# First rows' norm on ScalarE, postponed weight stores, output weights loaded in rows, separate PSUM kinds, and a planner that knows a shared port and longer DMA times

## The chip, the cores and the metric

The kernel runs on one core of a Trainium2 chip. Five engines work side by side, each on its own queue in program order: TensorE (PE; its weight loads are listed as PEld), VectorE (DVE), ScalarE (ACT), GpSimd (POOL) and SyncE (SP), which issues all DMAs here. Data lies in SBUF (128 partitions) and TensorE writes to PSUM, which has eight banks of 128 x 512 float32. The metric is the device time of one execution in microseconds; the time before is the median of three runs.

## What is computed

Two layers, each an attention block with a compressive memory and a Fourier mixing block, on x of 2048 rows by 512, in float32:

```python
for layer in range(2):
    x = x + A(layernorm(x))     # 32 heads of 16, four segments of 512 rows
    x = x + B(layernorm(x))

# A, per segment s, with q, k, v from wq, wk, wv and phi(t) = t + 1 if t > 0 else exp(t)
p = softmax(q_s @ k_s.T / 4 + causal mask)
a_mem = (phi(q_s) @ M) / (phi(q_s) @ z + 1e-6)
o_s = g * a_mem + (1 - g) * (p @ v_s)
M, z = M + phi(k_s).T @ v_s, z + sum(phi(k_s))
# then all o_s @ wo

# B
y = dft_seq_re @ (x @ dft_hid_re.T) - dft_seq_im @ (x @ dft_hid_im.T)
```

## The kernel before

**Numbers.** Products are made in float16 with each operand split into a high and a low half: three matmuls (high x high, high x low, low x high) stand for one. Every weight is scaled by a power of two from its absolute maximum first (`scales`, `split`, `split2`): maximum by VectorE, a transpose and a small matmul with ones on TensorE, a few operations on bits on VectorE; then ScalarE makes the high half, and VectorE or GpSimd the low half by a subtraction.

**Units of work.** Heads go in four groups of eight (`NG`), so a layer has 4 segments x 4 groups and the kernel 32 group units (`NGRP`). For a unit i:

- `s_p` projects queries and keys, `s_v` values; results go to a PSUM bank of kind `pj`, and `t_split` brings them to SBUF (ScalarE the high half, VectorE the low half), from where DMAs through DRAM (`d`) reorder them into `qst` and `kst` (three of each, `NR`).
- `s_x` makes all scores once to take each row's maximum (`t_max` on VectorE). They come in ten steps of 512 columns; the two halves of a step run side by side in two PSUM banks.
- `s_st` makes the transposed scores in ten more steps; `t_sel` takes the exponential (ScalarE) and masks (GpSimd).
- `s_av` multiplies with the values in two banks of kind `av`; `t_merge` transposes, divides by the denominators and is also used for the memory part (`s_mem`).
- `s_m` joins both parts into `ot`; after the four groups of a segment `s_o` multiplies with `wo`.

The mixing block takes over row by row: `s_ab` multiplies with the hidden matrices `wd`, `s_r` and `s_c` load and scale the sequence matrices, and `s_f` accumulates into `y`, one bank of kind `dft` at a time. The last quarter of the second layer uses sums of matrix blocks (`t_sums`, with the helper `ttw`) to save products (`t_win`).

**Order.** Nothing in the source says in which order these run. Each stage is a generator that yields what it needs next (`need`: engines, tiles read, PSUM or SBUF kinds to allocate). A planner (`class Plan`) estimates for every engine when it is free and for every tile when it is written and read, from costs per operation (`op`); the main loop always advances the generator that can go first. The instruction queues of the chip are written in that order once, before the run; on the chip each engine follows its queue and waits on semaphores. So a changed cost in `op` removes or adds no instruction and can still reorder all of them. `gate` holds a generator until named stages are planned; `tt` chooses between VectorE and GpSimd by the planned times.

**Slots.** PSUM's eight banks and 52 SBUF slots are lent by kind. `dict(pj=(1, 4), ...)` gives each kind a lowest number that others have to leave it and a highest number. `slots_free` says when a kind can have a bank. Before, maxima, scores and the small transposes of `scales` all use kind `ss`, (2, 6), and past four held `ss` banks two more must stay free.

**The first rows and weights.** Four tiles of x are loaded, then the query and key weights of groups 0 and 1 (into rows of `y`, used as a stage). `t_ln` normalises a row tile: statistics on VectorE, a power -0.5 on GpSimd (`rs`), the normalisation by a VectorE `tensor_scalar`, the high half on ScalarE, the low half on GpSimd or VectorE, and a transposing DMA into `xt`. `s_w` scales the weights: maxima of four pieces, `scales(0, 4)`, four parts, each followed by a store of the split weight to DRAM (`wqkv`, read again for later segments); when the first four row tiles are done it loads the value weights and the rest and goes on with `scales(4, 9)`. The first value projection needs that.

**The output weights.** `s_wo` loads `wo` (1 MB) with one DMA and `wd` (2 MB) with another once their stage rows are free, takes twelve maxima on VectorE, makes two scales one after the other, and splits 4 + 8 pieces.

Of the kernel before, what the change touches and what calls it, by code (L numbers as in the profile page):

```python
# [17 lines left out]
L = S // NSEG  # L18
# [22 lines left out]
AGAIN, LEAN = 0.0, 8.0  # L41
# [5 lines left out]
class Plan:  # L47
# [4 lines left out]
    def __init__(self):  # L52
# [6 lines left out]
        self.fresh = set()  # L59
        self.fine = {}  # L60
# [30 lines left out]
    def slots_free(self, kinds):  # L91
        extra, taken, r = {}, {}, 0.0
        for k in kinds:
# [14 lines left out]
            if k == "ss" and n >= 4:  # L108
                keep += 2
# [37 lines left out]
    def op(self, eng, name, args, kw):  # L147
# [61 lines left out]
        self.free[eng] = e  # L209
        if eng == "T":  # L210
# [47 lines left out]
def body(ctx: ExitStack, tc: tile.TileContext, x, wq, wk, wv, wo, beta, wd, cs, out):  # L258
# [141 lines left out]

    def s_w():
        def part(n, g, how):
# [123 lines left out]
    def t_ln(src, xi, dst, key, row=None):  # L526
# [4 lines left out]
        V.tensor_scalar(mv[:, 2:3], mv[:, 1:2], 1e-5, 2.0 ** -20, op0=OP.add, op1=OP.mult)  # L531
        yield need("G", mv)
        rs = rg("rs", 6, F32, (128, 1))
# [47 lines left out]
    def t_merge(e, o, gi, g, n, key):  # L581
# [843 lines left out]
```

## Time and profile before

| | |
|---|---|
| median of three runs | 1702.74 us (1701.61 to 1703.35) |
| the profiled execution | 1701.07 us |
| its span, first to last instruction | 1699.4 us |
| instructions | 32946 |
| mean granted TensorE clock | 0.986 |
| DMA traffic | 228.16 MB, 134 GB/s |

Times in views of the trace count from the span's start. All instructions but a few carry line 251, that of the helper that records them, so groups are told apart by the names of their tiles: `w` stands for any SBUF slot, `b` for a PSUM bank, `g` for `xt`, `amax` and `scl` for maxima and scales. A row of the order of time gives its start, how long it lasts, engine, line, operation, what it writes and reads, its form, how many are merged in it, and in brackets how long the engine was idle before and what ended that.

### The profile page before, as it was taken

The page shows a single profiled execution, that of the slowest core. Times are in us where ns is not written, and L with a number is a line of the kernel's source. Part 1 is how long each engine was busy: PE and PEld are TensorE (multiplying, and loading weights), DVE is VectorE, ACT ScalarE, POOL GpSimd, SP SyncE. Part 2 cuts the span into 40 slices and gives each one's busy share as a digit, 9 for nine tenths or more (in the row PEclk, how much of TensorE's full clock was granted, in tenths as well). Part 3 has the DMA queues.
Part 4 walks back from the last instruction along what each step waited for, and adds up shares of the span by engine and source line. Part 5 has one row for each costly group of instructions (what it writes and reads, how often), then busy time and mean ns, then how long its engine had stood idle before and what let it go on. Part 6 is the DMA issues. An engine that isn't in the chain of part 4 may idle for free.

```text
span 1699.4 us, 32946 instructions
## 1 busy us (share of the span) xinstructions
PE 1634.7 (96%) x11324; PEld 765.8 (45%) x11324; DVE 1176.6 (69%) x3630; ACT 865.5 (51%) x1433; POOL 839.2 (49%) x1287
## 2 busy tenths in 40 slices
PE   4988899999999999999899999999999999999999
PEld 2443343444445343444444444344444443444488
DVE  6887777778777877456488876857686765552266
ACT  3657656756654556544365664455445444430341
POOL 6547545555554554444345554334643533472672
PEclk9999899999999999999999999999999999999999
DMA  8673546535356433345856664334345331335263
GB/s 206 174 183 91 154 108 157 153 109 163 106 131 183 141 119 100 113 118 170 241 153 182 187 178 116 86 101 130 86 112 145 91 73 63 100 87 169 90 184 118
DMA packets 221272, 228.16 MB, mean 134 GB/s; under 512 B 113072, under 2 KB 139696, under 8 KB 221104
## 3 DMA queue, kind: packets, MB, share of 16 engines
q1 hardware_dynamic: 221104, 226.06, 47.7%
q8 instruction: 89, 1.46, 0.4%
q14 instruction: 79, 0.65, 0.1%
HBM read 140.51 MB, written 61.87 MB: 119 GB/s over the span
## 4 chain that ended last, share of the span: by engine, by line
PE 79%; DVE 7%; DMA 4%; ACT 4%; issue 3%; POOL 2%; SPq 1%; POOLq 0%; ACTq 0%; DVEq 0%
PE b L251 79%; ACT w L251 4%; DMA w<-w 2%; DVE w L251 2%; DVE junk L251 2%; POOL w L251 1%; DMA w<-in_cs_dram 1%; SPq L251 1%; DVE y L251 1%; DVE cam L251 1%; DVE bst L251 0%; DVE mx L251 0%; DMA y<-in_wv_dram 0%; DVE amax L251 0%; DMA kst<-d 0%
## 5 line engine op out<-in xcount | busy, mean ns | idle before, releaser
L251 PEld LDWEIGHTS <-w 128*128 128x128 f16 x5280 | 491.1, 98 | 570.8 <-issue 100.0
L251 PE MATMUL b<-w,w 128*128 128x512 f16 (+1 forms) x3360 | 698.5, 359 | 2.6 <-POOL w L251 1.0
L251 POOL TENSOR_TENSOR w<-w,w 128x512 f16<-128x512 f32 (+3 forms) x356 | 397.0, 1125 | 285.7 <-ACT w L251 246.0
L251 ACT ACTIVATE w<-b,fac 128x512 f32<-128x512 f32 x664 | 408.8, 695 | 174.3 <-PE b L251 173.6
L251 DVE CUSTOM_DVE_ANT_0 junk<-b,cmask 128x256 bf16<-128x256 f32 (+3 forms) x1024 | 437.1, 483 | 56.5 <-PE b L251 55.9
L251 POOL TENSOR_SCALAR_AFFINE_SELECT w<-w 128x256 f32<-128x256 f32 (+1 forms) x640 | 230.0, 368 | 284.8 <-ACT w L251 270.4
L251 DVE SCALAR_TENSOR_TENSOR y<-b,fyu,y 128x512 f32<-128x512 f32 (+1 forms) x296 | 202.1, 688 | 194.5 <-PE b L251 193.9
L251 ACT ACTIVATE w<-w,csu 128x512 f16<-128x512 f32 x320 | 225.5, 720 | 99.0 <-DVE csu L251 48.6
L251 ACT ACTIVATE w<-w 128x512 f16<-128x512 f32 (+2 forms) x160 | 99.5, 626 | 226.4 <-DVE w L251 179.0
L251 PE MATMUL b<-g,w 128*128 128x512 f16 x768 | 186.8, 386 | 3.3 <-DMA g<-w 2.6
L251 PE MATMUL b<-wd,w 128*128 128x512 f16 x768 | 181.5, 382 | 0.7 <-DMA w<-w 0.7
L251 PE MATMUL b<-w,vt 128*32 128x512 f32 (+3 forms) x2048 | 167.7, 450 | 0.2
L251 ACT ACTIVATE w<-b 128x512 f16<-128x512 f32 (+1 forms) x128 | 76.4, 598 | 151.3 <-PE b L251 143.7
L251 DVE SCALAR_TENSOR_TENSOR w<-b,w 128x512 f16<-128x512 f32 x120 | 82.1, 685 | 81.4 <-ACT w L251 81.3
L251 PE MATMUL b<-kst,qst 62*128 62x256 f16 (+3 forms) x1024 | 113.8, 302 | 11.6 <-ACT w L251 4.0
L251 POOL TENSOR_TENSOR w<-w,dn 128x256 f32<-128x256 f32 x109 | 66.3, 628 | 105.8 <-DVE dn L251 84.7
L251 PE MATMUL b<-qst,kst 64*128 64x512 f16 (+3 forms) x1024 | 113.5, 304 | 4.5 <-DVE mx L251 2.0
L251 PE MATMUL b<-w,g 128*128 128x128 f16 x1536 | 97.4, 222 | 5.7 <-DMA w<-w 2.2
L251 PEld LDWEIGHTS b<-w,vt 128*32 128x32 f32 x2048 | 59.9, 111 | 87.2 <-issue 59.0
L251 PEld LDWEIGHTS <-g 128*128 128x128 f16 x1536 | 90.7, 99 | 17.6 <-issue 11.8
L251 DVE STREAM_TRANSPOSE w<-b 128x512 f32<-128x512 f32 x112 | 74.2, 695 | 20.4 <-PE b L251 20.2
L251 PE MATMUL b<-wo,w 128*128 128x512 f16 x384 | 85.5, 379 | 0.0
(101 smaller groups left out, 1000.8 us busy)
## 6 DMA issues: line engine op xcount, KB each, us to landing
w<-in_cs_dram SPq DMA_DIRECT2D x160, 256.0 KB, 3.4
cc<-w SPq DMA_DIRECT2D x128, 256.0 KB, 2.7
w<-cc SPq DMA_DIRECT2D x112, 256.0 KB, 3.3
w<-w SPq DMA_DIRECT2D x96, 256.0 KB, 3.2
d<-w SPq DMA_DIRECT2D x128, 128.0 KB, 2.5
w<-in_x_dram SPq DMA_DIRECT2D x32, 256.0 KB, 3.7
qst<-d SPq DMA_DIRECT2D x64, 128.0 KB, 2.7
kst<-d SPq DMA_DIRECT2D x64, 128.0 KB, 2.9
```

The source lines that it names most:

```text
L251: r = f(*args, **kw)
```

## The change

1. **First rows.** For the four tiles of the first segment of the first layer, the normalisation goes to ScalarE, as an Identity activation with a scale and a bias per row. VectorE turns the sign of the mean, and GpSimd makes the bias, -mean times rs.
2. **Weight stores.** The stores of the split query and key weights of groups 0 and 1 go to a generator of their own (`keep`) that waits until the keys of unit 0 are planned; their SBUF slots are given back after store and projection, and the kind `wt` may hold five slots instead of three.
3. **Output weights.** `wo` and `wd` are loaded in twelve pieces of 128 rows by 512 columns (256 KB). Piece k is issued when more than k - 2 maxima are planned; each maximum is a task of its own (`peak`).
4. **PSUM kinds.** The maxima get the kind `sx`; scores and the small transposes stay with `ss`. Both have (2, 4) until group 3's attention is planned, then `ss` (2, 6) and `sx` (0, 6). The rule that joins two steps if four banks are to be had looks at each kind by itself.
5. **Merge.** The denominators are scaled into the PSUM bank that was transposed last and read from there by the reciprocal; that bank is given back after it.
6. **Sums of blocks.** `ttw` always takes GpSimd, where it chose between the two engines.
7. **The planner.** VectorE's operations on SBUF alone (`tensor_tensor`, `tensor_scalar`, `tensor_copy`, `scalar_tensor_tensor`) and GpSimd's operations other than `iota` and `memset` exclude each other in the plan. DMA issue and tail times, rate, and some estimates change.

```diff
@@ Plan.__init__, slots_free
+        self.port = dict(V=(0.0, 0.0), G=(0.0, 0.0))
...
-            if k == "ss" and n >= 4:
+            if k in ("ss", "sx") and n >= 4:
                 keep += 2
@@ Plan.op
+        shares = eng == "G" and name not in ("iota", "memset") or eng == "V" and not psum and name in (
+            "tensor_tensor", "tensor_scalar", "tensor_copy", "scalar_tensor_tensor")
+        if shares:
+            a, b = self.port["VG"[eng == "V"]]
+            if a <= t < b:
+                t = b
...
+        if shares:
+            self.port[eng] = t, e
...
-            issue, tail = self.dma or (440, 350 if stored else 950)
+            issue, tail = self.dma or ((370, 750) if stored else (450, 1000))
             if kw.get("transpose"):
-                issue, tail = 1350, 450
+                issue, tail = 1300, 800
...
-            self.free["D"] = max(self.free["D"], self.free["H"] + 650) + out[0].nbytes() / 360
+            self.free["D"] = max(self.free["D"], self.free["H"] + 650) + out[0].nbytes() / 310
@@ body
-    pl.setup(psum, "b", 8, dict(pj=(1, 4), av=(0, 2), dft=(1, 2), ss=(2, 6)))
+    pl.setup(psum, "b", 8, dict(pj=(1, 4), av=(0, 2), dft=(1, 2), ss=(2, 4), sx=(2, 4)))
...
-        en=(1, 1), wt=(2, 3), wv=(1, 2), craw=(4, 8), cc=(4, 8), pt=(8, 12), ot=(4, 8), xb=(2, 4),
+        en=(1, 1), wt=(2, 5), wv=(1, 2), craw=(4, 8), cc=(4, 8), pt=(8, 12), ot=(4, 8), xb=(2, 4),
@@ s_w
+    used = set()
+
+    def keep(n, g, w):
+        yield gate(("dk", 0))
+        yield need("Y", w)
+        Y.dma_start(wqkv[g][n], w)
+        yield lambda: (n, g) in used
+        pl.close(w)
...
-            yield need("Y", w)
-            Y.dma_start(wqkv[g][n], w)
             wnow[n, g] = w
             done.add(("W", n, g))
+            if g < 2 and n < 2:
+                spawn(keep(n, g, w))
+            else:
+                yield need("Y", w)
+                Y.dma_start(wqkv[g][n], w)
@@ s_wo
-        Y.dma_start(wos, wo.rearrange("(t p) n -> p t n", p=128))
-        yield gate(("W", 0, 3), ("W", 1, 3))
-        Y.dma_start(wds, wd.rearrange("(t p) n -> p t n", p=128))
...
-        for i in (12, 13, 14, 15, *range(8)):
-            yield need("V", y[:, i, :])
-            V.tensor_reduce(pm[:, (i + 4) % 16:(i + 4) % 16 + 1], y[:, i, :], axis=AX.X, op=OP.max,
-                            apply_absolute_value=True)
+        seen = []
+
+        def peak(k, row):
+            yield need("V", row)
+            V.tensor_reduce(pm[:, k:k + 1], row, axis=AX.X, op=OP.max, apply_absolute_value=True)
+            seen.append(k)
+
+        for k in range(12):
+            if k == 4:
+                yield gate(("W", 0, 3), ("W", 1, 3))
+            yield lambda: len(seen) > k - 2
+            row = y[:, (k + 12) % 16, :]
+            yield need("Y")
+            Y.dma_start(row, wo[128 * k:128 * k + 128] if k < 4 else
+                        wd[128 * (k // 2 - 2):128 * (k // 2 - 2) + 128, 512 * (k % 2):512 * (k % 2) + 512])
+            spawn(peak(k, row))
+        yield lambda: len(seen) == 12
@@ t_ln
+        first = key[:2] == ("L", 0)
+        if first:
+            V.tensor_scalar(mv[:, 0:1], mv[:, 0:1], -1.0, None, op0=OP.mult)
...
-        G.tensor_tensor(rs, mv[:, 2:3], mhalf, op=OP.pow)
-        yield need("V", rs)
-        V.tensor_scalar(xi, src, mv[:, 0:1], rs, op0=OP.subtract, op1=OP.mult)
+        G.tensor_tensor(rs[:, 0:1], mv[:, 2:3], mhalf, op=OP.pow)
+        if first:
+            G.tensor_tensor(rs[:, 1:2], mv[:, 0:1], rs[:, 0:1], op=OP.mult)
+            yield need("A", rs)
+            A.activation(xi, src, AF.Identity, bias=rs[:, 1:2], scale=rs[:, 0:1])
+        else:
+            yield need("V", rs)
+            V.tensor_scalar(xi, src, mv[:, 0:1], rs[:, 0:1], op0=OP.subtract, op1=OP.mult)
@@ t_merge
-            pl.close(p)
+            if p is e:
+                pl.close(p)
         dn = rg("dn", 4, F32, (128, 2, 16))
+        dm = o[:, 0:32].rearrange("p (a b) -> p a b", a=2)
...
-                V.tensor_scalar(dn[:, a], den, f, None, op0=OP.mult)
+                V.tensor_scalar(dm[:, a], den, f, None, op0=OP.mult)
...
-        V.reciprocal(dn, dn)
+        V.reciprocal(dn, dm)
+        pl.close(o)
@@ s_p
-                pl.close(w)
+                if i < 2:
+                    used.add((n, i))
+                else:
+                    pl.close(w)
@@ s_x (ps("ss") becomes ps("sx") throughout), and a new stream
+    def s_psum():
+        yield gate("WO")
+        pl.floor("dft", 1)
+        yield gate(("E", 3))
+        kinds = pl.area["ss"]["kinds"]
+        kinds["ss"], kinds["sx"] = (2, 6), (0, 6)
@@ ttw (and "VG" becomes "G" in the needs of t_sums)
-        E = min((V, G), key=lambda e: pl.free[e.key] + (LEAN if e is V else 2.0) * out.free_size())
-        E.tensor_tensor(out, a, b, op=op)
+        G.tensor_tensor(out, a, b, op=op)
@@ main loop
-                if w[2][:2] == ("ss", "ss") and r + EARLY >= other:
-                    both = pl.ready(w[1], w[2] + ("ss", "ss"), w[0])
+                if w[2][:2] in (("ss", "ss"), ("sx", "sx")) and r + EARLY >= other:
+                    both = pl.ready(w[1], w[2] + w[2][:2], w[0])
```

More of the change, by code (lines that the diff above doesn't have):

```diff
@@ L40 @@
 BATCH = 4
-AGAIN, LEAN = 0.0, 8.0
+AGAIN = 0.0
 FIRST = "cc", "craw"
@@ L642, in t_split @@
             if order:
-                Y.dma_start(o[0:32], f, est=(420, 1300))
-                Y.dma_start(o[32:48], f[0:16], est=(420, 1300))
-            else:
-                Y.dma_start(o[0:16], f[0:16], est=(420, 1300))
-                Y.dma_start(o[16:48], f, est=(420, 1300))
+                Y.dma_start(o[0:32], f, est=(430, 1450))
+                Y.dma_start(o[32:48], f[0:16], est=(430, 1450))
+            else:
+                Y.dma_start(o[0:16], f[0:16], est=(430, 1450))
+                Y.dma_start(o[16:48], f, est=(430, 1450))
         done.add(key)
@@ L819, in s_x @@
             for step in steps([128 * (t + 1) for t in range(TT)], (1,), (0, 2), (3,)):
-                yield need("T", qs, ks, tag=("ss", "ss"), mode="h")
-                sp = [ps("ss"), ps("ss")]
+                yield need("T", qs, ks, tag=("sx", "sx"), mode="h")
+                sp = [ps("sx"), ps("sx")]
                 for p, t, o, n in step:
@@ L829, in s_x @@
             yield lambda: left[0] == 0
-            yield need("T", mx, tag="ss")
-            pm = ps("ss")
+            yield need("T", mx, tag="sx")
+            pm = ps("sx")
             T.transpose(pm[0:32, 0:128], mx.rearrange("q a p t -> q (a p t)"), identf)
@@ L1088, in ttw @@
     def ttw(out, a, b, op):
[L1089 to L1090 removed]
+        G.tensor_tensor(out, a, b, op=op)
     def t_sums(a, b, d, c, j, t):
         lo, hi = slice(0, 256), slice(256, 512)
[L1094 removed]
+        yield need("G", a, b)
         ttw(d[:, lo], b[:, lo], b[:, hi], OP.add)
[L1096 removed]
+        yield need("G", a, d)
         ttw(d[:, hi], d[:, lo], a[:, lo], OP.subtract)
[L1098 removed]
+        yield need("G", a, b)
         ttw(a[:, lo], a[:, lo], b[:, lo], OP.subtract)
         pl.close(b)
[L1101 removed]
+        yield need("G", a, d)
         ttw(a[:, hi], a[:, hi], d[:, hi], OP.subtract)
@@ L1109, in t_sums @@
             A.activation(x, x, AF.Copy, scale=c)
-            yield need("VG", o, x)
+            yield need("G", o, x)
             ttw(o[:, 1], x, o[:, 0], OP.subtract)
@@ L1245, in s_f @@
         ar["kinds"]["ss"] = 2, 4
+        ar["kinds"]["sx"] = 0, 4
         wk = pl.area["cc"]["kinds"]
@@ L1328, in t_out @@
             Y.dma_start(fins[1][t + i], y[:, t + i, :])
-    streams = [[None, s()] for s in (s_r, s_c, s_st, s_ln, s_w, s_x, s_mem, s_v, s_p, s_ab, s_f, s_wo, s_k, s_b)]
+    streams = [[None, s()] for s in (s_r, s_c, s_st, s_ln, s_w, s_x, s_mem, s_v, s_p, s_ab, s_f, s_wo, s_k, s_b, s_psum)]
     hots += [[None, s()] for s in (s_m, s_o, s_av,)]
```

12 lines of the change are left out of this document (4 added, 8 removed).

## The prediction

> **What bounds the kernel now.** I read the page first, then the busy time by stages, then the first 45 us and the making of the output weights in order of time.
>
> ```profile
> span 1699.4 us, 32946 instructions
> PE 1634.7 (96%) x11324; PEld 765.8 (45%) x11324; DVE 1176.6 (69%) x3630; ACT 865.5 (51%) x1433; POOL 839.2 (49%) x1287
> ...
> PEclk9999899999999999999999999999999999999999
> ```
>
> TensorE is busy 1634.7 of 1699.4 us, so 64.7 us are idle. The stages say where (columns: stretch, its length, busy PE, PEld, DVE, ACT, POOL, clock, DMA share, GB/s).
>
> ```profile
> 0.00:18.00 18.00, 0.96 (x3) 0.58 (x3) 13.93 (x37) 5.81 (x9) 14.38 (x21) 1.00 0.71 175
> 18.00:40.00 22.00, 13.95 (x62) 6.58 (x63) 13.52 (x48) 8.76 (x16) 10.21 (x11) 0.87 0.86 235
> 40.00:100.00 60.00, 55.24 (x470) 30.48 (x467) 50.90 (x213) 37.08 (x63) 32.24 (x52) 0.90 0.69 177
> 100.00:200.00 100.00, 86.17 (x652) 39.61 (x649) 75.70 (x262) 64.03 (x108) 54.10 (x87) 0.90 0.48 127
> 200.00:300.00 100.00, 95.00 (x659) 40.44 (x657) 78.81 (x257) 63.63 (x107) 55.35 (x89) 0.98 0.55 142
> 300.00:800.00 500.00, 496.08 (x3285) 219.39 (x3284) 356.50 (x1059) 285.24 (x466) 254.68 (x378) 1.00 0.46 134
> 800.00:900.00 100.00, 94.60 (x632) 46.31 (x631) 66.96 (x219) 47.89 (x77) 41.88 (x53) 0.97 0.74 202
> 900.00:1500.00 600.00, 597.17 (x4335) 261.80 (x4335) 426.70 (x1387) 303.84 (x515) 279.18 (x489) 1.00 0.43 117
> 1500.00:1700.00 200.00, 195.52 (x1238) 120.62 (x1236) 93.61 (x156) 49.19 (x76) 97.14 (x111) 1.00 0.41 126
> ```
>
> Up to 18 us TensorE waits for its first operands (17.0 idle). From 18 to 40 it idles 8.1, from 40 to 200 another 4.8 + 13.8 = 18.6, and its clock stands at 0.87 to 0.90 all this time. From 200 to 1500 only 5.0 + 3.9 + 5.4 + 2.8 = 17.1 us are idle in 1300. So an edit pays in the first 200 us, or by changing what TensorE does when it is busy; other engines' work behind a full TensorE pays nothing.
>
> **The first rows and the first weights.** The start in order of time:
>
> ```profile
> 5.90 0.55 DVE L251 TENSOR_SCALAR w<-w,mv,rs 128x512 f32<-128x512 f32 x1 [0.23 <-POOL rs L251]
> ...
> 7.18 1.15 POOL L251 TENSOR_TENSOR w<-w,w 128x512 f16<-128x512 f32 x1 [0.70 <-ACT w L251]
> ...
> 7.37 1.25 DVE L251 TENSOR_SCALAR w<-w,mv,rs 128x512 f32<-128x512 f32 x1
> ...
> 10.13 0.66 DVE L251 TENSOR_SCALAR w<-w,mv,rs 128x512 f32<-128x512 f32 x1
> 10.47 0.73 POOL L251 TENSOR_TENSOR rs<-mv,mhalf 128x1 f32<-128x1 f32 x1
> ...
> 11.90 1.06 DVE L251 TENSOR_SCALAR w<-w,mv,rs 128x512 f32<-128x512 f32 x1
> ...
> 13.61 0.38 PE L251 MATMUL b<-identf,amax 128*4 128x128 f32 x1 [13.61 <-DVE amax L251]
> ...
> 17.49 3.61 SPq L251 DMA_DIRECT2D w<-w  x4
> ...
> 18.13 11.19 PE L251 MATMUL b<-g,w 128*128 128x512 f16 x45 [2.61 <-DMA g<-w]
> ...
> 18.57 0.71 ACT L251 ACTIVATE w<-y,scl 128x512 f16<-128x512 f32 x1
> ...
> 21.15 2.16 SPq L251 DMA_DIRECT2D y<-in_wv_dram  x4
> ...
> 24.27 0.69 DVE L251 TENSOR_REDUCE vm<-y 128x1 f32<-128x512 f32 x1 [2.64 <-DMA y<-in_wv_dram]
> ...
> 29.02 0.68 DVE L251 SCALAR_TENSOR_TENSOR w<-b,w 128x512 f16<-128x512 f32 x1
> ...
> 31.99 0.68 DVE L251 TENSOR_REDUCE amax<-y 128x1 f32<-128x512 f32 x1
> ...
> 32.73 0.27 PE L251 MATMUL b<-identf,amax 128*5 128x128 f32 x1 [3.41 <-DVE amax L251]
> ...
> 39.01 3.89 PE L251 MATMUL b<-w,g 128*128 128x128 f16 x35 [1.72 <-POOL w L251]
> ```
>
> Norm on ScalarE: VectorE loses 0.55 + 1.25 + 0.66 + 1.06 = 3.52 us (0.55 alone; 1.25 where GpSimd's 1.15 us subtraction ran beside it). It gains four sign flips of one column, at 0.18 us each by the shortest small operation shown below, 0.7 in all. ScalarE gains four activations with column operands, 4 x 0.71 = 2.8 us, in a stage where it is busy 5.81 of 18. GpSimd gains four one-column products; the trace has none, so between that 0.18 and the 0.73 of the power on the same shape. I take 0.3, nearer the plain operation. Per row GpSimd then does 0.73 + 0.3 + 1.15 = 2.2 us, four rows 8.7, and becomes what sets the transposes. The first projection waits for the last transpose, so it gains between 0 and 3.52 - 0.7 = 2.8 us; I take the middle, 1.4.
>
> Four stores put off: SP's queue loses 3.61 us ahead of the value weights' load, so this leaves 21.15 - 17.49 = 3.66 us sooner, and 1.4 more with the earlier transposes: 5.1. What waits for it moves along: VectorE idles 2.64 for that load with the first keys' split (29.02) queued behind it, the last maximum ends at 32.67, its transpose starts at 32.73, the first value projection runs from 39.01. The 6.3 us between the last two are a chain of small operations that stays. TensorE's own work ends at 18.13 + 11.19 = 29.3, or 27.9 afterwards. So 39.01 becomes about 34.0: **5.0 us**, the first 1.4 included. Bounds: 1.4, if the loads still land late at a DMA share of 0.86, and 6.5 with the whole 2.8. The stores come again once the first keys are written, next to those of later weights, with 1 MB in a stretch whose DMA share is 0.69; that hides them, and uncovered they give 3.6 us back.
>
> The clock after this gap:
>
> ```profile
> 30.00:40.00 10.00, 2.76 (x17) 1.92 (x18) 7.05 (x25) 4.97 (x10) 3.62 (x3) 0.72 0.82 201
> 40.00:50.00 10.00, 10.00 (x95) 7.38 (x93) 7.38 (x37) 7.12 (x11) 7.51 (x7) 0.76 0.84 245
> ```
>
> It costs 0.28 x 2.76 + 0.24 x 10 = 3.2 us. The gap shrinks from about 7.8 to 4.3, and I take the loss down in that proportion: **1.5 us** (0 to 3.2).
>
> **Output weights in rows, PSUM kinds.** In order of time, and then the page's DMA issues (count, size, us to landing):
>
> ```profile
> 92.51 0.51 SPq L251 DMA_DIRECT2D y<-in_wd_dram  x1
> ...
> 103.78 4.84 DVE L251 TENSOR_REDUCE pmax<-y 128x1 f32<-128x512 f32 x8 [3.11 <-DMA y<-in_wd_dram]
> ...
> 124.99 0.27 PE L251 MATMUL b<-identf,amax 128*1 128x128 f32 x1
> ...
> 189.46 1.16 POOL L251 TENSOR_TENSOR wd<-y,wd 128x512 f16<-128x512 f32 x1 [0.97 <-ACT y L251]
> ```
>
> ```profile
> w<-in_x_dram SPq DMA_DIRECT2D x32, 256.0 KB, 3.7
> ...
> y<-in_wd_dram SPq DMA_DIRECT2D x1, 2048.0 KB, 11.2
> ```
>
> VectorE stands 3.11 us in front of the 2 MB load with attention maxima queued behind, the maxima end at 108.62, yet their scale is transposed only at 124.99, for which a bank of kind "ss" must be free; the weights are ready at 190.6. Until then TensorE has only the first groups' attention and projections. The change removes the head-of-line wait, lets the scales ask in a kind that the maxima no longer fill, and writes the order by longer DMA times and by the lock between VectorE and GpSimd. Against it: with two rows in flight, twelve loads take 6 x (3.7 + 0.68) = 26 us where load and maxima took 108.62 - 92.51 = 16.1. The Trainium skill speaks against this part: "DMA: Bandwidth & Descriptors", section "Bandwidth", asks for 1 MiB or more per DMA, and its "Anatomy of one DMA" puts a fixed 2.0 us on each (both for DMAs issued from GpSimd, where these come from SP); an estimate from these pages is 6 x (2.0 + 0.6) = 16 us, no later than today, and the sum would stand; no run here shows these row loads yet.
>
> The stretch 100 to 200 loses 13.8 idle and 0.10 x 86.17 = 8.6 by its clock, 22.4 in all. The trace doesn't show the new order, so bounds: -2.2 (10 us later at that loss share), and 12, about half. I take a quarter, **5.5 us**, since the weights come with group 3's attention and not alone.
>
> **Steady state, merge, tail.** From the order of time, the tile of the denominators (shortest/median/longest ns) and the groups from 1440 us on (busy us, mean ns):
>
> ```profile
> 59.87 0.61 PE L251 MATMUL b<-kst,qst 62*128 62x256 f16 x8
> ...
> 61.93 0.39 PE L251 MATMUL b<-kst,qst 62*128 62x128 f16 x4
> ```
>
> ```profile
> L251 DVE TENSOR_SCALAR dn<-w,gb x112: 180/232/1189, 87.8 to 1489.9; 128x16 f32<-128x16 f32 x112
> ```
>
> ```profile
> L251 DVE TENSOR_TENSOR w<-w,w 128x256 f32<-128x256 f32 x9 | 7.8, 873 | 10.8 <-POOL w L251 7.7 <-ACT w L251 3.1
> ```
>
> A step of scores run alone costs 0.39, two together 0.61, so joining two saves 0.17. There are 20 x 32 = 640 steps; separate kinds let maxima find four banks while scores hold two, but leave projections fewer. One step in ten either way is 32 x 0.17 = 5 us; I take **1.0** gained (-5 to 5). Of the 17.1 idle us from 200 to 1500, better DMA times and the lock may recover some: **1.5** (-4 to 4). The merge's denominators go through PSUM, off the lock that stretches 232 ns to 1189 at times; the bank stays half a microsecond longer; 0, behind TensorE's work. The last sums all go to GpSimd: nine VectorE operations, 7.8 us, hidden by a TensorE that is full to 1695 with GpSimd at 97 of 200; uncovered, some 7.
>
> **Sum.** 5.0 + 1.5 + 5.5 + 1.0 + 1.5 = 14.5. The profiled run took 1701.07, 1.7 more than its span and 1.7 less than the median shown: 1686.6 for it, **1688 us** for the median.
>
> **Rivals.** (a) *The front gain alone survives* because VectorE, 50.90 of 60 and 75.70 of 100, paces the first groups whatever TensorE does: 1702.7 - 5.0 = 1698. For it: those shares; against: 30 us of TensorE loss beside them are waits, not full engines. (b) *Row pacing makes the output weights late*: the 5.5 becomes -2.2, total 6.8, 1696. For it: the 26 us; against: they can start 5 us sooner. (c) *Slower: banks.* Until group 3's attention ends, kinds keep 2 + 2 + 1 banks, attention holds 2, so one is left for projections (three before). Each of 24 projections then waits for its drain, 0.71 on ScalarE and 0.68 on VectorE, 1.4 us. Half of them uncovered cost 12 x 1.4 = 17; less 6.5 at the front, and nothing else gained, 1713. It decides when more than five wait with nothing else to run. For it: TensorE already lacks work there; against: attention holds its banks only in part of that time, and scores and maxima can fill. (d) *No change*: the stores come back at a bad place (3.6) and the new order loses the rest: 1702.
>
> **Chances.** Forecast 0.57, (a) 0.10, (b) 0.07, (c) 0.18, (d) 0.08. Faster by over 0.2% (3.4 us, about what such runs can tell from none): 0.74; within: 0.08; slower: 0.18. The forecast's own range is 1676 to 1697. Its best ends, 6.5 + 3.2 + 12, reach 1681, and a few joined steps 1676; to hold 8 in 10, the low end is 1675 and the high end 1707, into (c) where a few projections wait.
>
> **What would show it.** First projection near 16.7, the value weights' load before 17, first value projection near 34, clock above 0.8 from 30 to 50. No VectorE wait of 3 us on the large weights, the scale transposed before 115, output weights ready before 185, the stretch 100 to 200 busier than 90. Runs of four score matmuls fewer than before. I am wrong if TensorE waits on drains of projections before 190 us, if the output weights are later than 190, or if idle time from 200 to 1500 grows past 20.

## The result, and the profile after

The changed kernel takes **1710.03 us** (median of five runs; 1707.78 to 1713.17), the kernel before 1702.74 (five runs too): a ratio of 1.0047, 95% interval 1.0032 to 1.0061. The forecast was 1688 with 1675 to 1707: wrong in sign, and outside the range. The profiled execution has a span of 1708.3 us, 8.9 more than before. Busy time by stages (columns as before):

```profile
0.00:18.00 18.00, 1.38 (x5) 0.76 (x6) 12.54 (x45) 10.54 (x15) 15.22 (x26) 1.00 0.74 186
18.00:40.00 22.00, 19.32 (x119) 10.31 (x117) 13.25 (x39) 8.79 (x16) 11.73 (x13) 1.00 0.83 228
40.00:100.00 60.00, 51.33 (x436) 25.11 (x439) 51.76 (x217) 35.52 (x62) 29.49 (x50) 0.91 0.69 186
100.00:200.00 100.00, 85.38 (x663) 36.70 (x664) 80.34 (x283) 68.59 (x116) 59.88 (x100) 0.88 0.46 123
200.00:300.00 100.00, 98.07 (x679) 41.91 (x678) 68.55 (x214) 67.38 (x113) 57.71 (x90) 1.00 0.50 138
300.00:800.00 500.00, 490.71 (x3198) 217.63 (x3197) 360.57 (x1064) 272.17 (x448) 247.72 (x363) 0.99 0.46 131
800.00:900.00 100.00, 94.17 (x613) 46.02 (x612) 67.02 (x213) 45.84 (x75) 40.19 (x48) 1.00 0.73 201
900.00:1500.00 600.00, 595.65 (x4349) 261.71 (x4348) 422.82 (x1386) 306.61 (x521) 284.68 (x502) 1.00 0.43 118
```

From 18 to 40 us TensorE is busy 19.32 us where it was 13.95, and its clock is 1.00. From 40 to 100 it has 3.9 us less than before, and 100 to 200 is no better. From 200 to 1500 it idles 1300 - 1278.6 = 21.4 us (17.1 before).

Busy time hides slow and poorly packed matmuls, so the kernels are compared by a **loss**: the time elapsed minus the work done by then, each matmul counted at its full pace by its rows (512 float16 columns in 0.213 us, by the row `96.37 2.76 ... x12` quoted further down: eleven such steps and a last one of its own; float32 at half that pace, 192 columns every 0.162 us; score halves, and the 64-row products with the memory, run in pairs and count half; the 32-column products at 0.112 us for 512). The work is 1471.9 us in every kernel here, so equal loss at one time means equal progress. These are sums over all matmul rows, no view of the profile, and two executions of one order differ in them by up to 2.5 us:

| us | before | after | difference |
|---|---|---|---|
| 0 to 50 | 32.2 | 25.0 | -7.2 |
| 50 to 150 | 33.6 | 45.8 | +12.2 |
| 150 to 250 | 30.8 | 21.9 | -8.9 |
| 250 to 1500 | 123.8 | 136.4 | +12.6 |
| 1500 to the end | 7.2 | 7.4 | +0.2 |
| all | 227.6 | 236.5 | +8.9 |

So at 250 us the changed kernel is 3.9 us ahead: a gain at the front, a new loss behind it of which most comes back. What makes it slower is spread over the long steady part.

**The front**, in order of time after:

```profile
5.94 0.19 POOL L260 TENSOR_TENSOR rs<-mv,rs 128x1 f32<-128x1 f32 x1
6.17 0.81 ACT L260 ACTIVATE w<-w,rs 128x512 f32<-128x512 f32 x1 [1.26 <-POOL rs L260]
...
15.59 2.25 SPq L260 DMA_DIRECT2D y<-in_wv_dram  x4
...
17.58 9.38 PE L260 MATMUL b<-g,w 128*128 128x512 f16 x33 [4.27 <-DMA g<-w]
...
27.86 0.27 PE L260 MATMUL b<-identf,amax 128*5 128x128 f32 x1 [0.90 <-DVE amax L260]
...
33.41 2.78 PE L260 MATMUL b<-w,g 128*128 128x128 f16 x47 [1.78 <-POOL w L260]
```

```profile
30.00:40.00 10.00, 8.22 (x77) 5.70 (x75) 3.90 (x16) 6.59 (x12) 4.66 (x4) 1.00 0.86 254
40.00:50.00 10.00, 9.53 (x114) 5.92 (x113) 9.68 (x53) 8.63 (x15) 7.57 (x7) 1.00 0.90 231
```

The value weights are fetched 5.56 us sooner, the first value projection runs at 33.41 instead of 39.01, and the clock no longer falls after it.

**50 to 150 us.** VectorE, SP and TensorE after:

```profile
90.15 0.69 DVE L260 TENSOR_REDUCE pmax<-y 128x1 f32<-128x512 f32 x1 [1.17 <-DMA y<-in_wo_dram]
...
104.26 1.27 DVE L260 TENSOR_REDUCE pmax<-y 128x1 f32<-128x512 f32 x2
...
108.93 0.64 DVE L260 BATCH_NORM_STATS2 bst<-w 128x6 f32<-128x512 f32 x1
```

```profile
69.82 0.60 SPq L260 DMA_DIRECT2D w<-in_x_dram  x1
78.06 1.73 SPq L260 DMA_DIRECT2D qst<-d  x4
...
83.05 0.64 SPq L260 DMA_DIRECT2D w<-in_x_dram  x1
...
87.19 1.05 SPq L260 DMA_DIRECT2D y<-in_wo_dram  x2
...
90.76 4.63 SPq L260 DMA_DIRECT2D y<-in_wd_dram  x8
95.68 0.33 SPq L260 DMA_DIRECT2D w<-in_x_dram  x1
...
115.17 2.65 SPq L260 DMA_TRANSPOSE g<-w  x2
```

```profile
58.47 1.47 PE L260 MATMUL b<-g,w 128*128 128x512 f16 x6
...
113.32 1.34 PE L260 MATMUL b<-kst,qst 62*128 62x128 f16 x5 [3.86 <-DVE mhl L260]
...
128.65 2.12 PE L260 MATMUL b<-g,w 128*128 128x512 f16 x9
...
131.90 0.27 PE L260 MATMUL b<-identf,amax 128*1 128x128 f32 x1
```

The low halves of `wd`, a row of that tile's view (first and last start):

```profile
L260 POOL TENSOR_TENSOR wd<-y,wd x8: 1155/1159/1162, 158.0 to 181.8; 128x512 f16<-128x512 f32 x8
```

The second segment's last row tiles are loaded at 83.05 and 95.68 us, one behind a query load for which SP stands from 70.4 to 78.06, the other behind eight rows of `wd`; their statistics on VectorE come after all twelve maxima of the output weights and the attention maxima between these, at 108.93, and their transposes at 115.17. Between 59.9 and 128.65 TensorE has no projection of queries or keys to put between scores; before, the next one came at 105.37, and the four loads went out at 65.99, 69.89, 73.99 and 82.33. The output weights themselves are in time: the first maximum waits 1.17 us, not 3.11, the last low half ends at 181.8 + 1.16 = 183.0, and the first matmul with `wo` runs at 182.6 (197.3 before).

### The profile page after: what moved, and what is told of

The parts are those of the page before. It is cut to its first block, busy times and chain, and to the rows that moved or that the text cites. A ratio compares the mean times of both kernels' runs of the same rounds, so it can differ in the third digit from the quotient of the medians.

```text
span 1708.3 us, 33012 instructions
## 1 busy us (share of the span) xinstructions
PE 1640.5 (96%) x11324; PEld 765.1 (45%) x11324; DVE 1174.4 (69%) x3617; ACT 867.9 (51%) x1437; POOL 848.4 (50%) x1304
## 4 chain that ended last, share of the span: by engine, by line
PE 77%; DVE 8%; issue 5%; ACT 4%; POOL 3%; DMA 2%; SPq 1%; ACTq 0%; POOLq 0%; DVEq 0%
PE b L260 77%; ACT w L260 4%; DVE junk L260 2%; POOL w L260 2%; DVE w L260 1%; SPq L260 1%; DVE y L260 1%; DMA w<-w 1%; DVE cam L260 1%; DMA w<-in_x_dram 0%; DVE mx L260 0%; DVE bst L260 0%; DMA w<-in_cs_dram 0%; DMA y<-in_wv_dram 0%; POOL rs L260 0%
## 5 line engine op out<-in xcount | busy, mean ns | idle before, releaser
L260 PEld LDWEIGHTS <-w 128*128 128x128 f16 x5280 | 493.8, 98 | 566.7 <-issue 88.2
L260 POOL TENSOR_TENSOR w<-w,w 128x512 f16<-128x512 f32 (+3 forms) x364 | 403.9, 1120 | 304.0 <-ACT w L260 285.8
L260 DVE CUSTOM_DVE_ANT_0 junk<-b,cmask 128x256 bf16<-128x256 f32 (+3 forms) x1024 | 439.0, 483 | 61.2 <-PE b L260 59.9
L260 PE MATMUL b<-kst,qst 62*128 62x256 f16 (+3 forms) x1024 | 124.3, 304 | 15.4 <-DVE mx L260 4.8
```

The source lines that it names most:

```text
L260: r = f(*args, **kw)
```

## The experiments

A kernel's profile is one execution and may lie up to 5 us from its median; times below are medians, with the ratio to the kernel before in the same batch (1701.1 to 1701.9) and its 95% interval. What a run takes after 250 us is its median less 1473.6 (the work, and 1.7 outside the span) less its loss at 250: 132.5 before, 143.7 after. The expectations were written with a first count of the loss, in which float32 matmuls had a quarter of the pace; where they name a loss, the tables give that count too, in brackets (82.2 after and 81.8 before, at 250 us, and 64.0 and 57.0 at 150).

### Parts of the change taken out

**e1_peaks_last**: the maxima ranked last.

```diff
-            spawn(peak(k, row))
+            spawn(peak(k, row), lows)
```

> The changed kernel with one word more: the twelve maxima of the output weights are put into the list that the planner asks last, so the four row tiles of the second segment come ahead of them on VectorE. Theory (the late rows cost the front gain): the first projection of unit 4 starts before 112 us (128.7 changed, 105.4 before), TensorE's lost time at 150 us is about 7 less than in the changed kernel, and the time is 1700 to 1704. Rival 1 (the PSUM kinds cost it) and rival 2 (the planner's new times cost it, spread over the steady state): the projection moves, but the time stays at 1707 to 1713.

**e2_no_rows**: the two large loads and the maxima in the stream of the weights, as before; all else changed.

> The changed kernel with the output weights loaded by the two old DMAs and their maxima taken in the old stage. On VectorE only the last of the four row tiles comes after some of the maxima. Late-rows theory: most of the loss goes, 1701 to 1706. Both rivals: 1707 to 1713.

**e3_no_psum**: one kind `ss` (2, 6) as before; all else changed.

> The changed kernel with one PSUM kind for maxima and scores, as before. The order on VectorE then has all four row tiles ahead of the maxima. Late-rows theory and rival 1 (PSUM kinds) both expect 1700 to 1705; this run against e1 tells them apart: under late rows alone the two agree within 2 us, under rival 1 e1 stays near 1710 and this falls. Rival 2 (planner): 1707 to 1713.

**e4_front_only**: the kernel before with the first norm on ScalarE and the postponed stores.

> The kernel before with two parts alone: the first rows' norm on ScalarE and the four stores put off. If the front gain of about 7 us at 50 us lasts to the end: 1695 to 1698. If VectorE paces the first groups and takes it back whatever the order is: 1700 to 1704. If the order that follows from it costs by itself: above 1705.

| | median | ratio | loss at 150 | at 250 | after 250 |
|---|---|---|---|---|---|
| e1 | 1713.95 | 1.0076 (1.0057 to 1.0095) | 55.5 | 102.7 | 137.7 |
| e2 | 1700.16 | 0.9995 (0.9982 to 1.0007) | 64.0 | 87.0 | 139.6 |
| e3 | 1707.15 | 1.0033 (1.0022 to 1.0044) | 64.1 | 92.1 | 141.5 |
| e4 | 1700.18 | 0.9994 (0.9981 to 1.0006) | 67.7 | 95.0 | 131.6 |

In e1 the fourth unit's projection is back at 105.4, and the loss at 150 falls from 70.8 to 55.5. But its maxima now end at 150.28, and the first matmul with `wd` moves from 198.4 to 241.0: one late thing takes the place of the other, and 250 us is reached 10 us later. Without the row loads (e2) there is less of both: the projection comes at 112.7, the first matmul with `wd` at 208.7 (211.0 before). But its last two row tiles are loaded at 81.4 and 93.0 us, nearly as late as in the changed kernel, so the rows of `wd` are not what holds these loads back. And with one PSUM kind (e3), where the row loads and their tasks stay, all four tiles are loaded by 70.5 us and the projection runs at 96.8: the tasks alone don't make the tiles late.

Of the expectations, e1 lies above all its ranges and e2 a microsecond under the late rows' range; e3 lies in the range of the planner's new times (1707 to 1713), which no run tried alone; e4 lies in the band for a front gain that is taken back.

e4 shows how. It has nothing but the front, and it is 6.9 us ahead of the kernel before at 50 us (loss 25.3 against 32.2), 0.6 at 100 (48.9 against 49.5) and 1.9 behind at 150 (67.7 against 65.8). In order of time, and by stretches:

```profile
56.08 3.41 PE L260 MATMUL b<-g,w 128*128 128x512 f16 x15
63.09 0.40 PE L260 MATMUL b<-identf,mx 128*32 128x128 f32 x1 [3.60 <-DVE mx L260]
```

```profile
60.00:70.00 10.00, 5.02 (x30) 3.54 (x31) 6.72 (x29) 3.21 (x6) 2.96 (x3) 0.83 0.53 132
70.00:80.00 10.00, 8.83 (x31) 1.83 (x32) 9.86 (x47) 7.57 (x14) 5.14 (x12) 0.50 0.32 107
```

TensorE is through with the projections at 59.5 us, waits 3.60 us for the maxima of scores, and has the half clock from 70 to 80. Before, projections lasted until 69.1 us between the scores; from 60 to 80 TensorE was busy 9.94 and 8.71 us, at full clock. The changed kernel, too, has 1.8 of its 7.2 us left at 70 us (32.9 against 34.7) and 2.5 at 90 (41.1 against 43.6), when the first maximum of the output weights runs. So 4.7 of the 12.2 us that it loses from 50 to 150 come before those maxima. The front's 7 us are in all four runs at 50 us, and neither e2 nor e4 is measurably faster than the kernel before.

### The rows by themselves, and an order that differs in nothing else

**e5_rows_stream**: row loads, two ahead, each maximum in the stream (the edit is shortened).

```diff
-            spawn(peak(k, row))
+            yield need("V", last)    # the row loaded two steps earlier
+            V.tensor_reduce(pm[:, k - 2:k - 1], last, ...)
```

> The changed kernel with its twelve row loads, two in flight, but each maximum taken inside the weights' own stream (the place where the kernel before had them, behind the stream of the row tiles) and not as a task of its own. Theory (the rank of the maxima is at fault, not the loads): fourth unit's first projection by 115 us instead of 128.65, first transpose of amax before 140, first matmul with wd by 205, the loss by 250 us about 10 us smaller than after's, time 1700 to 1703. Rival (twelve loads in turn are too slow whatever the rank): the output weights come late as with the maxima ranked last, first matmul with wd past 220, time 1707 or more.

**e6_front_psum**: the kernel before with items 1, 2 and 4 of the change.

> The kernel before with three parts of the change: first norm on ScalarE, stores put off, PSUM kinds for maxima and scores. Without the row loads, the lock, the DMA prices, the merge and the tail. Theory (the kinds are worth some 5 us, as their removal from the changed kernel suggests by its loss from 370 to 650): 1693 to 1697, below both kernels. Rival (the gain of the front is given back from 370 to 1500, whatever else is in): 1699 to 1703.

**e7_rows_only**: the kernel before with item 3 alone.

> The kernel before with the row loads and their maxima as tasks, and nothing else. Theory (the maxima go ahead of the row tiles on VectorE and the next unit's projections starve): fourth unit's first projection later than 120 us (105.37 before), time 1707 to 1712. Rival (the rows hurt only with the new lock and DMA prices in the order): projection near 105, time 1700 to 1704.

**e8_twice_1010**: the kernel before, with one constant of the planner's rule for joining score steps.

```diff
-TWICE, EARLY, BESIDE = 1000.0, 0.0, 1000.0
+TWICE, EARLY, BESIDE = 1010.0, 0.0, 1000.0
```

> The kernel before with one constant of the planner, the time for which a lone step of scores is held back, at 1010 ns instead of 1000; the work is the same, the order is another from about 80 us on. Theory (the order of before is a favourable one among many that the planner can give, so any other order gives back some us from 370 to 1500): loss from 370 to 1500 of 75 to 80 us instead of 70.3, time 1704 to 1711. Rival (orders are worth much the same, and what is given back belongs to the parts of the change): 1700 to 1703.

| | median | ratio | loss at 150 | at 250 | after 250 |
|---|---|---|---|---|---|
| e5 | 1716.80 | 1.0083 (1.0065 to 1.0100) | 56.8 | 105.8 (90.8) | 137.4 |
| e6 | 1720.14 | 1.0104 (1.0089 to 1.0119) | 75.0 | 100.0 | 146.5 |
| e7 | 1704.49 | 1.0020 (1.0009 to 1.0031) | 69.0 | 98.5 | 132.4 |
| e8 | 1695.87 | 0.9969 (0.9959 to 0.9980) | 66.5 | 90.0 | 132.3 |

e5 repeats e1: output weights starved, first `wd` matmul at 244.2. In e7 the projection comes at 98.2 and 250 us is reached 1.9 us later than before: alone, the rows hardly harm, as the rival said, though their maxima are tasks there too. e6 was to show what the kinds are worth and is 20 us slower than e4, where e3 had them cost 3 in the changed kernel: over the whole run no part is worth a fixed amount. Up to 150 us the two agree, and the kinds do cost there: 7.3 us in e6 (75.0 against 67.7), 6.7 in the changed kernel (70.8 against 64.1); by 250 it is 5.0 and 0.6. And e8, in which no work is changed, is **6 us faster**, against both of its expectations: the order alone moves the time about as much as the whole change.

### The same constant in both kernels

> The kernel before with the planner's holding time for lone steps of scores at 900 ns instead of 1000: the same work in another order from about 80 us on. Theory of the spread (the planner's order alone moves the time by some 10 us either way, and at 1010 it already gained 6): anywhere from 1693 to 1712, and the two orders of this batch differ by 4 us or more. Rival (1010 was an exception and orders are worth the same): 1700 to 1704.

> The kernel before with that holding time at 1050 ns. Theory of the spread and rival as for 900: 1693 to 1712 against 1700 to 1704.

> The changed kernel with that holding time at 900 ns: its first 130 us stay in the order of the changed kernel, with the maxima of the output weights ahead of the row tiles, and what follows is another order. Theory of the spread: 1698 to 1715, with the loss at 150 us as in the changed kernel (64) and the difference made after it. Rival (the change itself costs its 7 us wherever the order goes): 1708 to 1713, slower than every order of the kernel before.

> The changed kernel with that holding time at 1050 ns, the same first 130 us. Theory of the spread: 1698 to 1715, loss at 150 us of 64. Rival as for 900: 1708 to 1713.

| constant | before | after | difference |
|---|---|---|---|
| 1000 | 1702.74 | 1710.03 | +7.3 |
| 900 | 1696.84 (e9; ratio 0.9963, 0.9951 to 0.9975) | 1693.40 (e11; 0.9948, 0.9931 to 0.9965) | -3.4 |
| 1050 | 1713.47 (e10; 1.0065, 1.0046 to 1.0083) | 1706.98 (e12; 1.0026, 1.0013 to 1.0039) | -6.5 |

e9 lies inside the range of its theory, e10 1.5 us above it, e11 4.6 below, and e12 inside, 1.0 under its rival's. Four orders of the kernel before span 17.6 us, three of the changed one 16.6. The sign of the difference depends on the constant; the mean of the three is -0.9 us with a standard deviation of 7, for which a 95% interval from three values reaches some 18 us to either side, so an effect of the size at issue can't be told from three pairs. By parts:

| constant | before: at 150, at 250, after 250 | after: at 150, at 250, after 250 |
|---|---|---|
| 1000 | 65.8, 96.6, 132.5 | 70.8 (64.0), 92.7, 143.7 |
| 900 | 65.2, 88.2, 135.0 | 69.3 (62.4), 88.9, 130.9 |
| 1050 | 66.3, 89.5, 150.4 | 68.3 (61.5), 89.2, 144.2 |

The loss at 150 is higher in every order of the changed kernel, by 2 to 5 us, and made good by 250 in all three (-3.9, +0.7, -0.3). (The three changed ones have the same order up to 150 us, so they are nearer to one case than to three.) After 250 us the loss goes from 131 to 150, in no relation to the kernel: the changed one at 900 has the least, the kernel before at 1050 the most. The means of the three are 139.3 and 139.6; with the spans of the profiled executions in place of the medians they are 136.7 and 139.8, and with e8 as a fourth the kernel before has 137.6. So nothing here ties the 11.2 us (143.7 - 132.5) that made the changed kernel the slower one to its edits, and the spread is wide enough for that one order to be all of it; that some microseconds belong to the edits is not excluded.

What a bad order can be made of is seen in e10, which shares its order with e8 until about 450 us and then loses 18 us between 1000 and 1050, where e8 loses 4.5:

```profile
1027.11 0.39 PE L251 MATMUL b<-kst,qst 62*128 62x512 f16 x2
1032.24 0.40 PE L251 MATMUL b<-identf,mx 128*32 128x128 f32 x1 [4.75 <-DVE mx L251]
1033.16 2.72 PE L251 MATMUL b<-w,g 128*128 128x128 f16 x24 [0.52 <-DMA w<-w]
1035.67 9.59 PE L251 MATMUL b<-wo,w 128*128 128x512 f16 x37
```

```profile
1020.00:1030.00 10.00, 6.47 (x61) 2.34 (x59) 8.51 (x27) 4.54 (x9) 3.87 (x8) 1.00 0.54 132
1030.00:1040.00 10.00, 7.24 (x39) 4.38 (x40) 3.56 (x11) 2.03 (x4) 2.96 (x3) 0.66 0.53 158
```

The order placed the 37 matmuls with `wo` behind a transpose of maxima that VectorE had not finished; TensorE stands 4.75 us, and its clock from 1030 to 1040 is 0.66. The 20 us of these two stretches lose 10.8 of the 18; another 5.8 go from 1000 to 1010, with a wait of 3.37 us for a load.

### Where the front's gain goes

**e13_rows_gated** (and **e14** with 900): no `wd` row is loaded until the second segment's tiles are done.

```diff
-                yield gate(("W", 0, 3), ("W", 1, 3))
+                yield gate(("W", 0, 3), ("W", 1, 3), *[("L", 1, t) for t in range(TT)])
```

> The changed kernel, but the eight rows of the wd weights are loaded only when the four row tiles of the second segment are transposed, so their maxima can't stand in front of those tiles. Theory of the place (50 to 150 us loses 12 to 14 more than the kernel before for this one reason): fourth unit's first projection at 100 to 108 us (128.65), first matmul with wd by 212, loss at 250 us of 62 to 70 (82.2 in the changed kernel, 81.8 before). Rival (what starves the maxima starves the output weights again, as with the maxima ranked last): first matmul with wd past 220, loss at 250 us of 80 or more. The time is then that loss plus what the order gives after 250 us, 88 to 109 in the orders seen: 1682 to 1706 by the theory, 1697 to 1718 by the rival.

> The same with the planner's holding time at 900 ns, another order from about 240 us on. Theory of the place and rival as at 1000, up to 250 us with the same losses within 2 us; the times of the two differ by the order after 250 us alone, by 3 to 15 us.

**e15** is e2 with 900, **e16** is e4 with 900.

> The changed kernel without row loads, with the holding time at 900 ns. Theory of the spread: loss at 250 us of 72 to 77 (74.4 at 1000), the rest 88 to 109, 1691 to 1713, no rule for which. Rival (900 is the better constant whatever the kernel, as it was for the kernel before and for the changed one): 1688 to 1695.

> The kernel before with the first norm on ScalarE and the four stores put off, with the holding time at 900 ns. Theory of the spread: loss at 250 us of 72 to 81 (80.3 at 1000), the rest 88 to 109, 1690 to 1717. Rival (the front's 7 us are kept in any order): 7 us under the kernel before at 900, 1690 or less.

**e17_tiles_first**: the changed kernel with the stream of the row tiles ranked ahead of all tasks, and the tiles of the second segment too; **e18** is the same on e15.

```diff
-spawn(t_ln(..., gt if here else None))
+spawn(t_ln(..., gt if here else None), hots if q == 1 else tasks)
...
-for s in (s_r, s_c, s_st, s_ln, s_w, ...
-hots += [[None, s()] for s in (s_m, s_o, s_av,)]
+for s in (s_r, s_c, s_st, s_w, ...
+hots += [[None, s()] for s in (s_ln, s_m, s_o, s_av,)]
```

> The changed kernel with the second segment's row tiles ranked first, ahead of every task: their loads (61.81, 69.82, 83.05 and 95.68 us in the changed kernel, the third behind a key load that waits on SP's queue), and their norm on VectorE ahead of the maxima of attention and of the output weights. Theory of the place (these tiles are what 50 to 150 us waits for, and four loads and four norms in front delay nothing else by more than some 4 us): all four loads by 72 us, fourth unit's first projection by 100, loss at 100 us of 36 to 39 (42.1 in the changed kernel, 44.0 before), at 250 us of 68 to 74, below every order so far or level with the best (73.5). Rival (something else paces the stretch: the maxima that the tiles now delay): loss at 100 us of 41 or more, at 250 us of 76 or more. The time is then that loss plus 88 to 109: 1683 to 1711 by the theory, 1691 to 1720 by the rival.

> The same rank for the row tiles in the changed kernel without row loads, with the holding time at 900 ns. Theory of the place: loss at 100 us of 36 to 39 (40 to 42 without the rank), at 250 us of 66 to 73 (73.5 without it), time 1681 to 1706, the lower half if the order after 250 us is as good as without the rank (87.9). Rival: 73.5 or more at 250 us, 1690 to 1715.

| | median | ratio | loss at 100 | at 150 | at 250 | after 250 |
|---|---|---|---|---|---|---|
| e13 | 1714.87 | 1.0079 (1.0051 to 1.0107) | 47.6 | 63.0 | 102.1 (87.2) | 139.2 |
| e14 | 1703.13 | 1.0007 (0.9991 to 1.0022) | 47.6 | 61.8 | 100.5 (85.5) | 129.0 |
| e15 | 1692.60 | 0.9944 (0.9926 to 0.9962) | 46.2 (40.7) | 63.8 | 86.1 (73.5) | 132.9 |
| e16 | 1707.37 | 1.0036 (1.0019 to 1.0053) | 48.1 | 67.0 | 99.4 (85.1) | 134.4 |
| e17 | 1695.33 | 0.9971 (0.9955 to 0.9987) | 45.3 (39.8) | 65.6 | 84.6 (72.0) | 137.1 |
| e18 | 1713.31 | 1.0072 (1.0056 to 1.0088) | 45.4 (39.8) | 64.0 | 87.4 (74.8) | 152.3 |

e13 and e14 went the rival's way: each some 8 us better than the changed kernel with the same constant by 150, the `wd` matmuls at 239 and 238, and 9 and 12 us worse by 250. Their losses agree within 2 us up to 250 and the times differ by 11.7. e15 lies in the ranges of its theory and of its rival, and so decides nothing between them. e16 made e4 7 us slower: 900 is not the better constant whatever the kernel, though it was in the four other pairs; and its loss at 250 (85.1) is above the 72 to 81 that was expected.

e17 does what the theory of the place says, up to 250 us:

```profile
62.22 0.58 SPq L260 DMA_DIRECT2D w<-in_x_dram  x1
64.26 1.09 SPq L260 DMA_DIRECT2D w<-in_x_dram  x2
70.61 0.60 SPq L260 DMA_DIRECT2D w<-in_x_dram  x1
...
82.89 1.23 SPq L260 DMA_TRANSPOSE g<-w  x1
89.40 2.61 SPq L260 DMA_DIRECT2D y<-in_wo_dram  x4
```

```profile
89.41 0.81 PE L260 MATMUL b<-g,w 128*128 128x512 f16 x3
...
96.37 2.76 PE L260 MATMUL b<-g,w 128*128 128x512 f16 x12
```

All four loads are out by 70.61, ahead of the waiting query load, the last transpose follows at 82.89, the projection runs at 89.41, 39 us sooner, and the scale of `wo` is transposed at 113.2 (131.9). The loss at 250 us is 8.1 us under the changed kernel's, 12.0 under that of the kernel before, and the lowest of all here; under the best order of the kernel before (e9, 88.2) it is 3.6. At 100 us it is only 2.3 better, less than the 3 to 6 expected. e18 has the same losses up to 150, but at 250 it is 1.3 worse than e15, which goes to the rival, and then 152.3 from the order behind it, the highest of all, which puts its time above its theory's range. The rank moved its tiles just as far (last load 69.6 us for 93.0 in e15, projection 91.2 for 113.1), and by 150 us nothing came of it. So late tiles are not by themselves what costs 50 to 150 us; in e17, where the rows' maxima had stood in front of them, the rank helps by 3 to 5 us (65.6 at 150 against 68.3 to 70.8). Clearly under both kernels as they were (1702.74 and 1710.03) are e15, e11 (1693.40) and e17, but also the kernel before in two other orders, e8 (1695.87) and e9 (1696.84).

## Why the prediction was wrong

**The front was right up to 50 us, and the step that carried it to the end failed.** 5.0 + 1.5 were forecast, and 7.2 us less are lost by 50 us. The value projection came at 33.41 for 34.0, the loads at 15.59. Inside it two sizes were off, one each way: the first projection gained 0.55 us, not 1.4, and the clock stood at 1.00 from 30 to 50 us, so the whole 3.2 came and not half. The activation took 0.81 us for my 0.71, the one-column product 0.19 for 0.3. But the sum took these 6.5 us off the whole time, as if TensorE had other work ready for the time gained. It had not: with the front alone (e4) they are gone by 150 us and the kernel is 0.9 us faster at the end, no more than chance (ratio 0.9994, 0.9981 to 1.0006), and with 900 (e16 against e9) 10.5 us slower.

**The output weights: a step that failed.** The text said that the change "removes the head-of-line wait" on VectorE, and counted only who waited behind it. It did not ask what the twelve new tasks are put ahead of. The main loop ranks tasks ahead of streams, and the row tiles come from a stream. So the wait went (1.17 us for 3.11), the weights were ready at 183.0 for 190.6, inside the 185 I gave, and `wo` ran 15 us sooner; but 50 to 150 us lost 12.2 us more, with the next projections 23 us late, and the 8.9 regained by 250 leave 3.3 lost for the 5.5 gained that I took. Not all of the 12.2 is this step's: 4.7 are lost before its first maximum runs, and e4, with neither rows nor kinds, loses 8.8 more than the kernel before in the same stretch. My bound of -2.2 thought of late weights only. e1, e5, e13 and e17 show it: taking the maxima away from in front of the tiles takes off 5 to 15 us up to 150, and only e17 does so without making the weights late. The rank does its harm together with the rest of the change: in e3, with one PSUM kind, and in e7, with the rows alone, the same tasks leave the tiles in time. The kinds, which shared this term of the sum, cost some 7 us up to 150 us by e3 and e6. The stretch from 100 to 200 is 85.38 busy for "busier than 90", and the scale came at 131.9 for 115.

**The steady part: the bound that failed, and the sign with it.** "1.5 (-4 to 4)" from 200 to 1500 came out as 11 to 13 lost from 250 us on. It priced better DMA times, and its bounds left out that any change in the plan rewrites every queue. Idle time there grew to 21.4, past the 20 that I had named as refuting me. Counted over the matmul rows in order of start, runs of four score matmuls, one step alone, fell from 147 to 121 as forecast; but runs of eight, two steps joined, fell as well, from 123 to 113, and runs of two rose from 72 to 87. So the 1.0 us for joining did not come. With seven orders that differ by one constant spread over 20 us, no price in this stretch to a few microseconds could have been argued from the profile, and the range needed some 10 us more on each side for it.

**The rivals.** Rival (a), that only the front's gain survives, was too hopeful as well. Rival (c) named 1713 and the right sign, by a mechanism that the runs do not bear out, so as far as is shown this was luck: TensorE's waits for ScalarE's drains from 50 to 250 us are 5.0 us, 4.6 before, and with a single kind (e3) the kernel is still slower than before. The one run that may belong to it is e6, where the kinds come on top of e4; there the waits for maxima (8.8 us) are longer than those for drains (5.9). What the kinds do cost up to 150 us is therefore not explained. The merge and the last sums were put at 0, and the end from 1500 on indeed lost 7.4 for 7.2 us; the merge was not tried by itself.

**The row loads.** Against them stood the Trainium skill's "DMA: Bandwidth & Descriptors", section "Bandwidth" (1 MiB or more per DMA). The twelve 256 KB loads and maxima took from 87.19 to 105.53, 18.3 us, where the two large loads and their maxima took 16.1, and where I feared 26: by their own duration the small loads cost some 2 us. The estimate of 16 from the fixed cost in that page's section "Anatomy of one DMA" came near.

**What stays open.** By 250 us the change is 3.9 us to the good against one order of the kernel before and level with the other two; over the whole run three pairs don't tell it from nothing. What takes the front's gain back is seen in e4 alone, as a wait for maxima and a low clock; no run tried to keep it. Where after 250 us each order gains or loses was followed up in one place only (e10). What the lock and the DMA prices do alone was not tried: e2 and e15, which have them, lose 8 to 13 us less by 250 than e4 and e16, which lack them and three smaller parts.

## What to carry to other kernels

Where a planner writes the order, a change is priced in two parts: what it does in its place, which the trace can tell to a microsecond, and a new order everywhere behind it, which here spread the time over 20 us. Run both versions in several orders that differ in a constant that changes no work before crediting or blaming the edit, and keep the best order as a find of its own. When work becomes a task of higher rank, ask what it now stands in front of; and when a stage ends sooner, follow what the next stage needs, loads, tiles and maxima, since they must come sooner too.

## What the runs showed of the hardware

TensorE's clock fell to half without a long pause. In e6, by stretches of 10 us:

```profile
120.00:130.00 10.00, 8.49 (x94) 4.87 (x93) 9.43 (x39) 7.97 (x15) 4.26 (x11) 1.00 0.80 175
130.00:140.00 10.00, 8.73 (x42) 2.62 (x42) 7.91 (x35) 2.98 (x6) 3.85 (x6) 0.53 0.12 29
140.00:150.00 10.00, 7.80 (x28) 1.74 (x25) 10.00 (x55) 0.00 (x0) 0.00 (x0) 0.50 0.00 0
150.00:160.00 10.00, 7.94 (x47) 2.56 (x46) 4.06 (x18) 8.61 (x15) 4.05 (x9) 0.50 0.18 44
```

From 130 to 160 us the clock is 0.50 to 0.53, though matmuls start at most 0.7 us apart from 130 to 154 us by their rows (many are 0.69 apart, the time of one maximum on VectorE), and the longest idle time just before, at 129.7, is 1.4 us. What is low is their number, 28 to 47 where 94 ran just before; whether it is the number or the kind of matmul that counts isn't shown. The Trainium skill, "TensorE: Matmul & The Clock Gate", in its part on the HAM clock gate, ties the half clock to an idle window of about 3.4 us, and tells in the same part of a kernel whose frequent micro-idles between groups of matmuls made the clock swing. This trace is nearer to the second: work without such a window, but sparse, had the half clock for 24 us. So a stage that waits on maxima pays again in its clock: from 50 to 150 us e6 was idle 15.6 us, and lost some 16 more by its clock (the busy time of each 10 us times what its clock is short of 1).
